# Variance plus epsilon moved from GpSimd to VectorE, with new priorities for the stages of a four-layer kernel

## The chip, the cores and the metric

The kernel runs on one core of one Trainium2 chip. The metric is device time in microseconds (us) for the whole program. The engines are named as the profile names them: PE (TensorE, matrix products), DVE (VectorE), ACT (ScalarE), POOL (GpSimd) and SP (SyncE, which here only issues DMA transfers). PEld is PE's loading of weights, which runs beside its matmuls. Each engine works through its own list of instructions in order. An instruction may wait for counters (semaphores) that other instructions raise.

## The reference

The input x has 2048 rows of 576 numbers. Four layers follow each other, attention and feed-forward twice, with the same weights both times:

```python
x = x + _A_ref(_layernorm(x), A_wqkv, A_wo)
x = x + _B_ref(_layernorm(x), B_w1, B_b1, B_w2, B_b2)
x = x + _A_ref(_layernorm(x), A_wqkv, A_wo)
x = x + _B_ref(_layernorm(x), B_w1, B_b1, B_w2, B_b2)
```

`_layernorm` is `(x - m) / sqrt(v + 1e-5)`. `_A_ref` is attention with 32 heads of 18 numbers, in which a row sees itself and the 255 rows before it, followed by the projection `wo`. `_B_ref` normalises once more, multiplies by `w1` (576 to 4608), adds `b1`, applies gelu, multiplies by `w2` (4608 to 576) and adds `b2`.

## The kernel before

**Tiles and chunks.** A tile is 128 rows. A chunk is four tiles, so each pair of an attention and a feed-forward layer has four chunks, and the program has eight, k = 0 to 7. Chunks 0 to 3 belong to the first pair, 4 to 7 to the second.

**What is done for a chunk, by stage.** A stage has a name that ends in the number of its chunk:

- `ln k`: normalises the rows for attention. DVE makes statistics (L592) and joins them to mean and variance (L594). The function `ln_rstd` then makes 1/sqrt(v + eps) in two steps: variance plus epsilon into `vtmp` (L603), and that to the power -0.5 into `rstd` (L605). DVE scales the rows (L615), and an SP transpose brings them into `xnTa` (L635).
- `q k.i`: for tile i, the products q, k and v. Each is two sets of five matmuls (L671) into two banks of PSUM; DVE copies a bank out (L710 for q and k, L697 for v), and an SP transpose brings q and k into place (L729).
- `ea k`, `eb k`: attention of the head groups 0 to 3 and 4 to 7. A group has three units. In a unit PE makes scores (L757), ACT applies exp (L766), POOL masks (L787), and PE multiplies by v (L804). At the end of a group DVE divides (L814, L819). In chunk 0 the units are smaller, since there are no rows before it.
- `t k`: the tail. An SP transpose brings the result into `attT` (L848), PE multiplies by `wo` (L671 again, a helper's line), DVE adds to `x_res` (L838), and both normalisations that follow are done in one, by the same L592 to L615, with L620 for the last 64 columns and a transpose into `xnTm` (L635).
- `ga k`, `gb k`: first and second half of the product with `w1` (L881 for the last 64 rows, L893 for the rest) and gelu on ACT (L896).
- `ma k`, `mb k`: first and second half of the product with `w2` (L922), added to `x_res` by DVE (L838), or in the last layer into the output (L841).
- Names with a `+` are the loads of `w1`, `w2` and `x_res` that belong to a stage (L536).

**What sets the order.** Nothing is emitted at once. `add` records a task with its engine, what it reads and writes, a cost, a latency and a priority. Then `Plan.schedule` places all tasks in a modelled time: of the tasks that could start first, the one with the lowest priority number goes first. It also gives each task its bank of PSUM, and before 140 us of modelled time it puts warm-up matmuls (stage without a name, function `keep_warm`) into gaps of PE. The order found so is the list that each engine works through. The dictionary `PL.nudge` adds a number to the priority of all tasks of a stage; a stage that is not in it gets nothing added:

```python
stage = self.stage + ("+" if dma in ("w1", "w2", "xr") else "")
prio += self.nudge.get(stage, 0.0)
```

So a changed entry, or a changed engine, cost or latency of any task, can move instructions everywhere in the program, on all engines and in the queues of SP and POOL.

`ln_rstd` is called with one tile (the start and the tails, 36 times) or with four (`ln`, 7 times), 43 times in all.

Of the kernel before, what the change touches and what calls it, by code (L numbers as in the profile page):

```python
# [8 lines left out]
ALU = mybir.AluOpType  # L9
# [31 lines left out]
class Sched:  # L41
# [23 lines left out]
    def add(self, eng, fn, reads=(), writes=(), dma=None, ring=4):  # L65
        waits = {}

        def want(ev):
            c, v, _e = ev
            if waits.get(c, 0) < v:  # L70
                waits[c] = v

        for r in reads:
            lw = self.last_write.get(r)
            if lw is not None and not (eng == "pe" and lw[2] == "pe"):
                want(lw)
        for w in writes:
            for rd in self.readers.get(w, ()):
                if rd[2] != eng or rd[3]:
                    want(rd[:3])  # L80
            lw = self.last_write.get(w)
            if lw is not None and not (eng == "pe" and lw[2] == "pe"):
                want(lw)
        if dma is None:
            assert eng != "sp"
            c = self.cnt[eng]
            amount = 1
        else:
            rg = self.ring(eng, dma, ring)
            c = rg.sems[rg.i % rg.k]  # L90
            rg.i += 1
            amount = 16
            if c.val > 0:
                want((c, c.val, None))
        wl = []
        wd = self.waited[eng]
        for cc, v in waits.items():
            if wd.get(cc, 0) >= v:
                continue
            wd[cc] = v  # L100
            wl.append((cc, v))
        c.val += amount
        own = None if dma is not None else eng
        ev = (c, c.val, own)
        self.steps[eng].append(Step(eng, fn, wl, c, amount))
        for w in writes:
            self.last_write[w] = ev
            self.readers[w] = []
        for r in reads:
            self.readers.setdefault(r, []).append((c, c.val, own, dma is not None))  # L110
        return ev
# [297 lines left out]
def build_kernel(nc, A_x, A_wqkv, A_wo, B_x, B_w1, B_b1, B_w2, B_b2, out):  # L409
# [32 lines left out]
    PL = Plan(S, 7)  # L442
    add = PL.add


    PL.nudge = {"b": 1.83, "ea0": -1.98, "ld0+": 40.46, "eb0": 2.23, "q1.0": -6.02, "q1.1": 1.09, "t0": 6.35, "ga0": -26.49, "q2.0": 12.46,
                "q2.2": 12.06, "q2.3": 21.72, "t1": -35.56, "ea2": -3.78, "ga1": -4.7, "ma1": 15.69, "ma1+": -9.39, "q3.2": -1.65, "q3.3": -7.2,
                "eb3": 1.74, "ma2": 3.52, "q4.0": 39.31, "q4.2": 6.69, "q4.3": -1.19, "t3": 50.91, "mb2": 75.66, "mb2+": -12.34, "eb4": 2.23,
                "ma3": 19.38, "q5.3": 4.22, "t4": -3.2, "ln6": 1.17, "ga4": 2.93, "ma4": 3.37, "q6.0": 2.8, "q6.1": 2.68, "q6.3": 11.39, "t5": 14.34,
                "gb4": 5.24, "ln7": 19.99, "ea6": 18.52, "mb4": 22.88, "ma5": 16.32, "q7.0": 16.24, "q7.1": 29.31, "q7.2": 33.42, "q7.3": 24.98,  # L450
                "t6": 73.06, "gb5": 28.24, "mb5": 74.41, "ga6": -3.51, "eb7": -2.5, "t7": -1.07}

    def sb(name, shape, dtype):
        return nc.alloc_sbuf_tensor(name, shape, dtype)
# [21 lines left out]
    vtmp = sb("vtmp", [P, NT], FP32)  # L476
# [91 lines left out]
    for i in range(NQN):  # L568
        add("pool", lambda e, i=i: e.memset(qn[:, i, :].rearrange("p (h e) -> p h e", e=32)[:, :, DH:32], 0.0),
            writes=[f"qn{i}h{h}" for h in range(2)], cost=0.5, prio=-9)  # L570
# [26 lines left out]
    def ln_rstd(ts, fused, prio):  # L597
        t0, n = ts[0], len(ts)
        var = mv_all[:, t0:t0 + n, 1]
        mvs = [f"mv{t}" for t in ts]  # L600
        rds = [f"rstd{t}" for t in ts]
        sc, bi = (1.0 + EPS, EPS * EPS) if fused else (1.0, EPS)
        add("pool", lambda e: e.tensor_scalar(vtmp[:, t0:t0 + n], var, sc, bi, op0=ALU.mult, op1=ALU.add),  # L603
            reads=mvs, writes=[f"vt{t}" for t in ts], cost=0.2, lat=0.09, prio=prio)
        add("pool", lambda e: e.tensor_tensor(rstd[:, t0:t0 + n], vtmp[:, t0:t0 + n], nhalf[:, 0:n], ALU.pow),  # L605
            reads=[f"vt{t}" for t in ts] + ["nhalf"], writes=rds, cost=0.4 + 0.155 * n, lat=0.08, prio=prio)

# [236 lines left out]
    def tail(k, prio):  # L844
        l, t0, nt = CH[k]
        rd = [f"aq{g}" for g in range(G)]
        for i in range(nt):
            add("sp", lambda e, i=i: e.dma_start_transpose(attT[:, :, i * 128:(i + 1) * 128], attq[:, i, :]),  # L848
                reads=rd + ["aqd"], writes=[f"aT{i}"], dma="t", ring=8, cost=1.3, lat=0.6, move=0.72, desc=640, prio=prio - 0.1)
        for i in range(nt):  # L850
            t = t0 + i
            bs = two_out(lambda c, i=i: attT[:, c, i * 128:(i + 1) * 128], lambda c, s: wo_sb[:, c, s:s + HB],
                         [f"aT{i}", "woA", "woB", "woC"], prio)
            for o in range(2):
                resid(t, o, bs[o], prio)
            ln_stats(t, prio)
            ln_rstd([t], True, prio)
            ln_norm_T(t, i, xnTm[:, k % 2], f"xm{k % 2}_", prio, dup=True)
# [82 lines left out]
    def ln1(k, prio):  # L941
        l, t0, nt = CH[k]
        ts = list(range(t0, t0 + nt))
        ln_rstd(ts, False, prio)
        for i, t in enumerate(ts):
            ln_norm_T(t, i, xnTa, "xa", prio)
# [5 lines left out]
    for i in range(n0):  # L952
        ln_rstd([i], False, -20)
        ln_norm_T(i, i, xnTa, "xa", -6, x_in, [f"xin{i}"], pe=True)
    add("pool", lambda e: e.memset(vA[:, :, :, DH:VW], 1.0), writes=[f"v{s}h{h}" for s in range(VS) for h in range(2)], cost=0.7, reads=["rstd3"], prio=-5)
    xin_load(4, 4, ["xa3"], -6)
    for i in range(n0):
# [4 lines left out]
        cost=0.5, prio=-1)  # L962
    dma("sp", b2bc[:, :], bass.AP(tensor=B_b2.tensor, offset=B_b2.offset, ap=[[0, P], [1, D]]), reads=["k3"], writes=["b2"], cls="b", ring=2,
        cost=0.5, prio=-1)
    add("pe", lambda e: e.transpose(bank(bb).bitcast(BF16)[:, 0:NF], b1in[:, :], ident[0:NF, 0:NF]), reads=["b1i", "ident"], writes=[bb],
        cost=0.1, lat=0.22, prio=5, alloc=[bb])
# [24 lines left out]
    for k in range(NK + 1):  # L991
        b = 4 * k
# [64 lines left out]
def bass_interleave_layers__sliding_block__mixer_channel_mlp__prompt_kernel(  # L1057
    nc,
    A_x,
    A_wqkv,  # L1060
    A_wo,
    B_x,
    B_w1,
    B_b1,
    B_w2,
    B_b2,
    out,
):
    build_kernel(nc, A_x, A_wqkv, A_wo, B_x, B_w1, B_b1, B_w2, B_b2, out)
# [28 lines left out]
```

The softmax here doesn't subtract the row's maximum and nothing guards it: scores larger than these inputs give would overflow.

## Time and profile before

| | us |
|---|---|
| median of 4 runs | 927.55 (926.53 to 928.12) |
| the profiled execution | 929.88 |
| its span, first to last instruction | 927.8 |
| PE busy | 899.6 (97%) |
| ACT busy | 598.7 (65%) |
| POOL busy | 366.8 (40%) |
| DVE busy | 317.2 (34%) |
| L603 on POOL, 36 of one tile | 209 ns each |
| L605 on POOL, 36 of one tile, 7 of four | 587 and 1022 ns each |
| mean granted clock of PE | 0.998 |

The profile is one execution. A row of a group of instructions gives line, engine, operation, what is written and read, and the count; then busy time and mean duration of one in ns; then how long the engine stood idle just before, and what ended that. A row of the timeline gives start and duration, the same names, and in brackets how long the engine had stood idle and which instruction or transfer ended the wait. Rows of equal instructions that follow each other are merged. A stretch of matmuls counts as busy even where each is short, so the waits say more than the busy share.

### The profile page before, as it was taken

The numbers are of one execution on the slowest core, as the hardware profiler recorded it, in microseconds if no ns is written. First come the engines' busy times: TensorE is split into PE (matmuls) and PEld (weight loads), VectorE is DVE, ScalarE is ACT, GpSimd is POOL, SyncE is SP. The second block draws the span as 40 slices with busy tenths as digits, with TensorE's granted clock in tenths as the row PEclk, the third lists the DMA queues.
The fourth block names the chain that finished last, engine by engine and source line by source line (L and its number), as shares of the span: only waits on it lengthen the run. The fifth ranks groups of instructions, "written<-read, shape, count | busy, mean of one in ns | idle before, by whom it ended". The sixth has DMA issues, their size and how long they took to land. (4 is left out here: it accounts for less than half of the span.)

```text
span 927.8 us, 22424 instructions
## 1 busy us (share of the span) xinstructions
PE 899.6 (97%) x9374; PEld 566.4 (61%) x9411; DVE 317.2 (34%) x797; ACT 598.7 (65%) x721; POOL 366.8 (40%) x505
## 2 busy tenths in 40 slices
PE   8989899999999999999999999999999999999998
PEld 6556465575756757577564756656576564657556
DVE  5647211841334403176020723145123420241001
ACT  4877687677836777662777667656685777852541
POOL 3766444562613626061351644315443363610100
PEclk9999999999999999999999999999999999999999
DMA  8798839934196332852739451683619626184430
GB/s 195 122 213 136 190 113 201 223 118 132 35 208 166 117 115 95 189 104 48 226 42 273 73 170 61 168 196 60 202 41 209 156 56 216 31 211 147 155 115 26
DMA packets 204596, 128.85 MB, mean 139 GB/s; under 512 B 128848, under 2 KB 202448, under 8 KB 204496
## 3 DMA queue, kind: packets, MB, share of 16 engines
q1 hardware_dynamic: 199952, 120.06, 52.4%
q0 software_dynamic: 2112, 4.72, 2.1%
q10 hardware_dynamic: 2432, 2.65, 0.9%
q8 instruction: 74, 1.21, 0.6%
q14 instruction: 26, 0.21, 0.1%
HBM read 91.87 MB, written 2.36 MB: 102 GB/s over the span
## 5 line engine op out<-in xcount | busy, mean ns | idle before, releaser
L766 ACT ACTIVATE pT<-ps 128x1024 bf16<-128x1024 f32 (+2 forms) x384 | 348.8, 970 | 123.7 <-PE ps L757 122.6
L787 POOL TENSOR_SCALAR_AFFINE_SELECT pT<-pT 128x512 bf16<-128x512 bf16 (+1 forms) x368 | 282.0, 790 | 269.4 <-ACT pT L766 260.5
L922 PE MATMUL ps<-w_sb,hT 128*128 128x288 bf16 x2304 | 313.5, 286 | 1.5 <-DVE x_res L838 1.5
L896 ACT ACTIVATE hT<-ps,b1col 128x512 bf16<-128x512 f32 x288 | 198.0, 687 | 174.6 <-PE ps L893 173.0
L893 PE MATMUL ps<-xnTm,w_sb 128*128 128x512 bf16 x1115 | 255.0, 379 | 3.0 <-issue 1.7
L922 PEld LDWEIGHTS ps<-w_sb,hT 128*128 128x128 bf16 x2304 | 211.9, 97 | 71.3 <-issue 16.7
L893 PEld LDWEIGHTS ps<-xnTm,w_sb 128*128 128x128 bf16 x1152 | 108.8, 98 | 138.0 <-issue 17.4
L838 DVE TENSOR_TENSOR x_res<-ps,x_res 128x288 f32<-128x288 f32 x160 | 71.3, 450 | 235.3 <-PE ps L922 213.3
L671 PE MATMUL ps<-wqkv,xnTa 128*128 128x288 bf16 x960 | 135.9, 288 | 5.9 <-DVE qn L710 2.5
L671 PEld LDWEIGHTS ps<-wqkv,xnTa 128*128 128x128 bf16 x960 | 87.2, 98 | 39.8 <-DVE qn L710 7.6
L804 PEld LDWEIGHTS ps<-vA,pT 128*128 128x128 bf16 x2880 | 94.1, 96 | 25.7 <-POOL pT L787 12.2
L804 PE MATMUL ps<-vA,pT 128*128 128x20 bf16 x2880 | 100.0, 171 | 4.1 <-POOL pT L787 3.5
L710 DVE CAST qn<-ps 128x288 bf16<-128x288 f32 x120 | 54.2, 454 | 117.4 <-PE ps L671 116.9
L904 POOL TENSOR_TENSOR x_res<-x_res,b2bc 128x576 f32<-128x576 f32 x32 | 40.9, 1277 | 115.5 <-ACT hT L896 115.4
L757 PE MATMUL ps<-qT,kT 32*128 32x384 bf16 (+2 forms) x1216 | 64.2, 277 | 3.9 <-ACT pT L766 2.7
L814 DVE RECIPROCAL rinv<-ps 128x16 f32<-128x16 f32 x64 | 16.2, 253 | 129.1 <-PE ps L804 128.9
L603 POOL TENSOR_SCALAR vtmp<-mv_all 128x1 f32<-128x1 f32 (+1 forms) x43 | 8.9, 206 | 109.4 <-DVE mv_all L594 107.9
L592 DVE BATCH_NORM_STATS2 st_all<-x_res 128x6 f32<-128x288 f32 x104 | 44.8, 448 | 11.6 <-DMA x_res<-in_A_x_dram 10.1
L671 PE MATMUL ps<-wo_sb,attT 128*128 128x288 bf16 x320 | 45.0, 286 | 1.7 <-DMA attT<-attq 0.9
L881 PE MATMUL ps<-xnTm,w_sb 64*128 64x512 bf16 x288 | 39.5, 377 | 2.4 <-DMA xnTm<-xn 1.4
L615 DVE TENSOR_SCALAR xn<-x_res,mv_all,rstd 128x576 bf16<-128x576 f32 x52 | 36.6, 705 | 13.8 <-DMA xnTm<-xn 8.0
L757 PEld LDWEIGHTS ps<-qT,kT 32*128 32x128 bf16 x1216 | 19.5, 92 | 34.5 <-issue 18.6
(43 smaller groups left out, 284.7 us busy)
## 6 DMA issues: line engine op xcount, KB each, us to landing
w_sb<-in_B_w_dram SPq DMA_DIRECT2D x48, 864.0 KB, 6.2
w_sb<-in_B_w_dram SPq DMA_DIRECT2D x48, 768.0 KB, 4.8
w_sb<-in_B_w_dram SPq DMA_DIRECT2D x96, 48.0 KB, 4.6
x_res<-in_A_x_dram POOLq DMA_DIRECT2D x4, 1152.0 KB, 7.3
out_dram<-xn SPq DMA_DIRECT2D x16, 144.0 KB, 1.8
wqkv<-in_A_wqkv_dram ACTq DMA_DIRECT2D x3, 576.0 KB, 7.5
hT<-in_A_x_dram SPq DMA_DIRECT2D x2, 576.0 KB, 5.4
wo_sb<-in_A_wo_dram ACTq DMA_DIRECT2D x1, 576.0 KB, 6.6
```

The costliest lines, as they stand in the source:

```text
L592: add("dve", lambda e, i=i, s=s: e.bn_stats(st_all[:, t, i, :], s[:, t, i * HB:(i + 1) * HB]), reads=res, writes=[f"st{t}_{i}"], cost=0.37 ...
L671: ins = e.matmul(bank(bs[o])[:, 0:HB], lhs(c), rhs(c, o * HB), start=(c == 0), stop=(c == KD - 1))
L710: add("dve", lambda e, b=bs[o], dst=dst: e.tensor_copy(dst, bank(b)[:, 0:HB].rearrange("p (h d) -> p h d", d=DH)), reads=[bs[o]], writes=[ ...
L757: ins = e.matmul(two(bs[j // 2])[:, j % 2, col:col + nq * 128], k_of(T0 + so)[0][32 * j:32 * j + 32, g, :], qs[32 * j:32 * j + 32, g, qo * ...
L766: add("act", lambda e, h2=h2: e.activation(pT[:, sl, 2 * h2:2 * h2 + 2, lo:hi], two(bs[h2])[:, :, lo:hi], ACT.Exp, scale=SCALE), reads=[bs ...
L787: add("pool", lambda e, ap=ap, pat=pat, sgn=sgn, kind=kind: e.affine_select(ap, ap, pattern=pat, compare_op=(ALU.is_ge if kind == "d" else ...
L804: ins = e.matmul(bank(B_O)[:, o:o + VW], pT[:, sl, j, col + qi * 128:col + (qi + 1) * 128], vA[:, (T0 + so) % VS, 4 * g + j, :], start=(fi ...
L838: add("dve", lambda e: e.tensor_tensor(x_res[:, t, sl], bank(b)[:, 0:HB], x_res[:, t, sl], ALU.add), reads=[b], writes=[f"x{t}h{hh}"], cos ...
L893: ins = e.matmul(bank(bk)[:, 0:n], w1_sb[:, sl, col:col + 128], xnTm[:, k % 2, c, 0:n], start=False, stop=(c == 3))
L896: add("act", lambda e, ff=ff, fl=fl, bk=bk: e.activation(hT[:, fl, 0:n], bank(bk)[:, 0:n], ACT.Gelu_apprx_tanh, bias=b1col[:, ff:ff + 1]), ...
L904: add("pool", lambda e, t=t: e.tensor_tensor(x_res[:, t, :], x_res[:, t, :], b2bc[:, :], ALU.add), reads=["b2", f"h{fl}"], writes=X(t), co ...
L922: ins = e.matmul(bank(b)[:, 0:HB], hT[:, fl, i * 128:(i + 1) * 128], w2_sb[:, fl, hh * HB:(hh + 1) * HB], start=(fl == 0), stop=(fl == NFH ...
```

## The change

`ln_rstd` computes variance plus epsilon on DVE instead of POOL, with a modelled cost of 0.1 instead of 0.2 and a latency of 0.14 instead of 0.09. POOL keeps the power. And `PL.nudge` has other entries: 43 instead of 55.

```diff
-    PL.nudge = {"b": 1.83, "ea0": -1.98, "ld0+": 40.46, "eb0": 2.23, "q1.0": -6.02, "q1.1": 1.09, "t0": 6.35, "ga0": -26.49, "q2.0": 12.46,
...
-                "t6": 73.06, "gb5": 28.24, "mb5": 74.41, "ga6": -3.51, "eb7": -2.5, "t7": -1.07}
+    PL.nudge = {"b": 2.99, "ea0": 3.17, "q1.0": 4.26, "q1.1": 4.31, "q1.2": 4.01, "q1.3": 3.37, "ga0": -2.67, "q2.0": 14.64, "q2.1": 2.99,
...
+                "eb6": 0.91, "ma5": 10.07, "q7.1": -1.18, "q7.3": 7.71, "ea7": -15.2, "ga6": -19.72, "eb7": -2.14}
```

```diff
         sc, bi = (1.0 + EPS, EPS * EPS) if fused else (1.0, EPS)
-        add("pool", lambda e: e.tensor_scalar(vtmp[:, t0:t0 + n], var, sc, bi, op0=ALU.mult, op1=ALU.add),
-            reads=mvs, writes=[f"vt{t}" for t in ts], cost=0.2, lat=0.09, prio=prio)
+        add("dve", lambda e: e.tensor_scalar(vtmp[:, t0:t0 + n], var, sc, bi, op0=ALU.mult, op1=ALU.add),
+            reads=mvs, writes=[f"vt{t}" for t in ts], cost=0.1, lat=0.14, prio=prio)
         add("pool", lambda e: e.tensor_tensor(rstd[:, t0:t0 + n], vtmp[:, t0:t0 + n], nhalf[:, 0:n], ALU.pow),
             reads=[f"vt{t}" for t in ts] + ["nhalf"], writes=rds, cost=0.4 + 0.155 * n, lat=0.08, prio=prio)
```

The list of each engine changes in many places, up to a point near the end: the last 190 steps of PE are the same in both.

## The prediction

> **What bounds the kernel now.** I read the page first, then who PE waits for, then PE's timeline, and last PE against the other engines in chosen windows. The page says that PE is the bound:
>
> ```profile
> span 927.8 us, 22424 instructions
> PE 899.6 (97%) x9374; PEld 566.4 (61%) x9411; DVE 317.2 (34%) x797; ACT 598.7 (65%) x721; POOL 366.8 (40%) x505
> ```
>
> 927.8 less 899.6 leaves 28 us. The change adds and removes no matmul of the computation, so an order can win only from these 28 us, and lose by making more of them. Who PE waits for, longest in total first:
>
> ```profile
> PE ps L757 <- ACT pT L766: 4.1, 12, 1.1
> PE ps L804 <- POOL pT L787: 3.5, 8, 1.1
> PE ps L671 <- DVE qn L710: 2.8, 4, 1.2
> PE ps L671 <- DMA xnTa<-xn: 2.4, 1, 2.4
> ...
> PE ps L922 <- DVE x_res L838: 1.5, 5, 0.6
> PE ps L881 <- DMA xnTm<-xn: 1.4, 1, 1.4
> ...
> PE ps L671 <- DMA attT<-attq: 0.9, 1, 0.9
> ...
> PE ps L757 <- DVE mv_all L594: 0.8, 1, 0.8
> ```
>
> Columns: total, times, longest. They are small and many; none is a wait for rstd. Where they lie is seen in PE's timeline:
>
> ```profile
> 40.67 0.34 PE L757 MATMUL ps<-qT,kT 32*128 32x384 bf16 x4
> ...
> 45.08 0.34 PE L757 MATMUL ps<-qT,kT 32*128 32x384 bf16 x4
> ...
> 48.58 0.79 PE L671 MATMUL ps<-wqkv,xnTa 128*128 128x288 bf16 x5 [2.42 <-DMA xnTa<-xn]
> ...
> 53.45 0.34 PE L757 MATMUL ps<-qT,kT 32*128 32x384 bf16 x4 [0.16 <-ACT pT L766]
> ...
> 101.90 0.82 PE L881 MATMUL ps<-xnTm,w_sb 64*128 64x512 bf16 x6 [1.44 <-DMA xnTm<-xn]
> ```
>
> The windows show the same start with the granted clock (columns after the stretch: its length, then busy time of PE, PEld, DVE, ACT, POOL, then clock, DMA share, GB/s):
>
> ```profile
> 30.00:33.60 3.60, 2.65 (x56) 1.82 (x54) 3.15 (x11) 2.61 (x4) 1.28 (x3) 1.00 0.82 129
> 33.60:37.00 3.40, 3.29 (x28) 1.72 (x25) 1.97 (x8) 3.02 (x5) 2.64 (x5) 0.51 0.49 81
> 46.00:48.60 2.60, 0.18 (x3) 0.02 (x2) 0.46 (x1) 0.98 (x2) 2.11 (x4) 1.00 1.33 380
> ```
>
> In one stretch of 3.4 us the clock was 0.51: 3.29 us of PE work there would have taken half, so 1.6 us were lost. It follows a stretch in which PE had mostly short matmuls (36 of the 56 are L804, of 20 columns).
>
> **The moved operation.** Its chain, once, at the start:
>
> ```profile
> 4.44 0.21 DVE L594 BATCH_NORM_AGGREGATE mv_all<-st_all 128x2 f32<-128x12 f32 x1
> 4.73 0.19 POOL L603 TENSOR_SCALAR vtmp<-mv_all 128x1 f32<-128x1 f32 x1 [0.43 <-DVE mv_all L594]
> 5.01 0.56 POOL L605 TENSOR_TENSOR rstd<-vtmp,nhalf 128x1 f32<-128x1 f32 x1
> ```
>
> From the end of the aggregate (4.65) to the start of the power (5.01) 0.36 us pass. After, VectorE follows itself, which took 0.04 us between statistics and aggregate; then come its operation and a hop of 0.08 to GpSimd (4.65 to 4.73). VectorE's operation on 128x1 is not in the trace. Nearest rows:
>
> ```profile
> L603 POOL TENSOR_SCALAR vtmp<-mv_all 128x1 f32<-128x1 f32 x36 | 7.5, 209 | 90.2 <-DVE mv_all L594 89.0
> L594 DVE BATCH_NORM_AGGREGATE mv_all<-st_all 128x2 f32<-128x12 f32 x64 | 12.8, 200 | 0.7
> ```
>
> Below, VectorE's memset of 165 ns; above, its reciprocal of 253 ns. I take 0.20, the nearest in size: 0.04 + 0.20 + 0.08 = 0.32 instead of 0.36, so 0.04 us less per chain (0.075 less to 0.01 more). If all 43 chains lay on PE's path, that would be 1.7 us; no PE wait ends at rstd, so I count nothing: each chain is covered by fill matmuls, or ends in a late transpose priced below. GpSimd gets 8.9 us free of 367, and waits for ACT in long stretches anyway (L787: 260.5 us). Its power still stands in line behind masks, so in chains of four tiles (masks to 23.84 us, then L603 at 23.92) only the 0.28 us of L603 and its hop go. VectorE gets 43 x 0.20 = 8.6 us on top of 317: its 34% become 35%. What is queued behind the new instruction on VectorE are the evictions of PSUM banks. PE waited for VectorE some 12 times in about 440 evictions, so 43 x 12/440 x 0.2 = 0.2 us; with the gain on a few chains, this part is 0 (-1.7 to +1).
> [...]
>
> **The new order.** I counted PE's list in both programs. The work prices: five L671 matmuls 0.61 us (x30 from 14.05 to 17.78), six L922 0.74, four L893 0.86, scores of a unit 0.24 to 0.34, its L804 0.19 to 0.39, 0.09 for changing away from scores. By them the two lists weigh the same to half a us. Warm-up matmuls are 46 in both. SP issues the same 152 transposes (1.2 us each in its timeline) and 215 copies in another order; no PE wait ends at a weight load, and I price that at nothing: the least cover is 6.6 us of PE work between the release of a w2 slice and its first use (7.0 before), against 4.8 us to landing on the page; late, it would cost what lies above 6.6. The last 190 PE steps (from 784 us on) are the same. So the sum is one of waits.
>
> *Up to the first feed-forward block (101.9 us).*
> Goes: the 2.42 at 48.58 (from the last read of its tile of xnTa to the first use there were 3 units and 3 sets of L671, 3.85 us; now 24.8). The 1.44 at 101.90 (8.7 us of work after the last L671 of the tail; now 15.2): -3.86.
> Comes: the transpose for tile 2 of chunk 2 has 2.88 us of work to hide in (2 units, 2 sets). Before, 4.54 us were enough with no wait, and 3.85 were 2.42 short, so it needs at most 4.5 or as much as 6.3: 0 to 3.4 us. The first attT of the tail is in the same place with 4.1 us; it needed 4.18 + 0.89 = 5.07 in chunk 2, and its wait lies in the same time. PE is held up by ACT there too, so I take 1.5.
> Comes: attention of chunk 0 is thinner. Sets of L671 among the scores of head groups 1 to 7 were 3, 3, 3, 5, 5, 3, 4; now 1, 2, 3, 4, 3, 3, 3. PE work per group falls from 3.9 to 5.1 us to 2.5, 3.2, 4.3, 4.4, 4.2, 3.8, 3.8. The quickest group took 4.41 us (40.67 to 45.08, with 4.0 of work), so exp and masks allow about 4.4. After lacks 1.9 + 1.2 + 0.1 + 0 + 0.2 + 0.6 + 0.6 = 4.6, before 1.3. The first group of chunk 1 falls to 4.7, where the quickest full-size group took 6.18: +1.2. Net +4.5. Were the floor that of the groups of 5.8 us, it would be some 6 more; nothing less, since 4.41 is the best seen.
> Goes with it: 0.80 and 0.37 in chunk 0, now inside that floor, and half of the 0.31, 0.31, 1.15, 1.13 in chunk 1, which has 30 sets instead of 29 there: -2.6.
> Clock: group 1, with one set, is thinner than the stretch that brought 0.51; I take one such stretch again: 0 (-1.6 to +3.2).
> Sum -0.5.
> [...] Here the longest wait before the fall was 0.80, and the 2.42 us were followed by 1.00. [...]
>
> *From there to 784 us.*
> Goes, each where the list has changed: 0.89 (attT, 261.8), 0.99 (638.1), 0.59 (178.5), 0.37 (402.1), 0.51, 0.33, 0.30 (masks): -3.98.
> Comes: tile 1 of chunk 5 now has 2.93 us between the last read of xnTa and first use: 4.54 - 2.93 = 1.6 (0 to 3.4). The first tile of chunk 4 has 12.40 us from its last residual; 13.21 were 0.99 short in chunk 7, 12.42 were enough in chunk 5: 0.9 (0 to 1.8). Banks that come back late: +0.3. Mask waits fall where units meet little fill, and the list has as many such places: +1.1. Sum -0.1.
>
> Together -0.6. The profiled execution took 929.88 us (927.8 and 2.1 around), 2.3 above the median of 927.55; the difference is put on the median: **926.9**.
>
> **Rivals.** (a) *Slower: the clock falls more often.* Groups 1 and 2 of chunk 0 (about 30 to 40 us) and 6 to 8 (about 55 to 70) are thin in the new list. Every half-clock stretch with PE at the bound costs 1.6. Three more give 926.9 + 4.8 = 931.7; two more decide it (930.1). For: the one fall came after thin work. Against: ACT has PE waiting there anyway, and similar waits at 46 and 90 us cost no clock. (b) *Faster: the thin groups cost nothing*, because the start was late by chains, not by ACT: the -3.9 stay, +4.5 shrinks to 1: 923.4. Against: groups 3 and 6 stood at 4.4 and 4.7 with less PE work. (c) *The operation is no faster on VectorE*: 0.01 more per chain, nothing to see; the order alone decides, so this is inside all cases.
>
> **How the numbers follow.** Even exchange (924 to 930) 0.42; (a), 930 to 936, 0.33; (b), 919 to 924, 0.25. About 0.2%, 1.9 us, can be told from no change here: faster is below 925.7, slower above 929.4. Faster: 0.25 and 0.10 of the first; slower: 0.33 and 0.08; the rest 0.24. The range takes most of both sides, 920 to 935.
>
> **What would show it.** No PE wait at the second chunk's first L671, none of 1.4 at the first L881; waits of 1 to 2 at q2.2 (about 75 us) and at tile 1 of chunk 5 (about 450 us); L766 as the releaser of PE in 30 to 40 and 55 to 70 us; L603 on VectorE at about 0.2 us. Wrong if the first L881 starts far from 98 us, if the clock row has two or more stretches of 0.5, or if weight loads on SP's queue are waited for.

## The result and the profile after

| | before | after |
|---|---|---|
| median, us | 927.02 (46 runs, 924.53 to 929.98) | 930.93 (28 runs, 926.74 to 934.99) |
| after / before | | 1.0038 [1.0029, 1.0046] |
| profiled execution, its span, us | 929.88, 927.8 | 931.23, 929.4 |
| mean granted clock (before: 85 executions timed beside the experiments; after: its 28) | 0.9989 | 0.9943 |

The changed kernel is slower by 0.38%, where 926.9 us and an even exchange were forecast. 930.93 lies inside the range, on the side to which 0.41 had been given. The profiled execution of before was one of its longer ones: 929.88 against a median of 927.02. Lines of the changed kernel stand one lower than before (L671 is L670, L757 L756, L766 L765, L615 L614, L603 L602).

The page of after, with the span first and then the busy times:

```profile
span 929.4 us, 22415 instructions
PE 899.6 (97%) x9373; PEld 567.5 (61%) x9411; DVE 323.2 (35%) x840; ACT 598.1 (64%) x721; POOL 355.9 (38%) x462
PEclk9899999999999999999999999999999999999999
```

PE is still the bound. VectorE has 43 instructions and 6 us more, GpSimd 43 and 11 us less. The clock row has an 8 in the second slice, 23 to 46 us. The operation itself, in the groups of after (busy time, mean of one in ns):

```profile
L602 DVE TENSOR_SCALAR vtmp<-mv_all 128x1 f32<-128x1 f32 x36 | 5.2, 143 | 0.5
L602 DVE TENSOR_SCALAR vtmp<-mv_all 128x4 f32<-128x4 f32 x7 | 2.3, 328 | 0.2
```

It takes 143 ns where 200 were priced. Who PE waits for in after (total, times, longest):

```profile
PE ps L756 <- ACT pT L765: 4.9, 16, 0.6
PE ps L670 <- DVE qn L709: 4.4, 7, 2.3
...
PE ps L670 <- DMA attT<-attq: 1.8, 3, 1.3
PE ps L803 <- POOL pT L786: 1.6, 4, 0.7
PE ps L803 <- DVE attq L818: 1.5, 2, 1.2
...
PE ps L670 <- DMA xnTa<-xn: 1.1, 2, 0.8
```

The 2.4 for `xnTa` and the 1.4 for `xnTm` are gone, as forecast, and so is most of the wait for masks. Waits for exp rose from 4.1 to 4.9. One row was not forecast: PE waits for VectorE's copies of `qn`, once for 2.3 us. PE's timeline of after places the waits:

```profile
39.06 0.34 PE L756 MATMUL ps<-qT,kT 32*128 32x384 bf16 x4 [0.28 <-ACT pT L765]
41.68 0.99 PE L670 MATMUL ps<-wqkv,xnTa 128*128 128x288 bf16 x5 [2.28 <-DVE qn L709]
...
79.50 2.01 PE L670 MATMUL ps<-wo_sb,attT 128*128 128x288 bf16 x15 [1.33 <-DMA attT<-attq]
...
99.48 0.82 PE L880 MATMUL ps<-xnTm,w_sb 64*128 64x512 bf16 x6
...
458.12 3.83 PE L670 MATMUL ps<-wqkv,xnTa 128*128 128x288 bf16 x30 [0.76 <-DMA xnTa<-xn]
```

What VectorE does while PE stands still, from its timeline in after:

```profile
37.02 0.69 DVE L614 TENSOR_SCALAR xn<-hT,mv_all,rstd 128x576 bf16<-128x576 bf16 x1
37.63 0.44 DVE L818 TENSOR_TENSOR attq<-ps,rinv 128x288 bf16<-128x288 f32 x1
38.00 3.26 DVE L614 TENSOR_SCALAR xn<-hT,mv_all,rstd 128x576 bf16<-128x576 bf16 x3
41.18 0.44 DVE L709 CAST qn<-ps 128x288 bf16<-128x288 f32 x1
```

And GpSimd's in the same stretch:

```profile
38.39 0.97 POOL L535 DMA_DIRECT2D x_res<-in_A_x_dram  x1 [0.84 <-PE ps L756]
39.38 3.54 POOL L786 TENSOR_SCALAR_AFFINE_SELECT pT<-pT 128x1024 bf16<-128x1024 bf16 x5
```

Of the three scalings merged in the row at 38.00, the first two took 414 and 417 ns. The third started at 38.67, inside GpSimd's issue of the first `x_res` load, and took 2581 ns. The copy of a `qn` bank stood behind it on VectorE, and PE waited for that bank. In before the load stood at 42.21, behind the last scaling (41.02 to 41.76), and none of the four there took over 0.84 us.

The windows of after, cut at the half-clock stretches (columns as before):

```profile
30.00:35.30 5.30, 3.17 (x47) 1.78 (x44) 4.65 (x17) 5.30 (x8) 3.50 (x5) 1.00 0.74 101
35.30:38.70 3.40, 3.40 (x55) 1.96 (x52) 2.31 (x7) 2.20 (x4) 2.51 (x4) 0.50 0.42 82
38.70:42.10 3.40, 0.84 (x11) 0.45 (x9) 2.92 (x3) 2.26 (x4) 3.38 (x5) 1.00 0.70 171
42.10:45.50 3.40, 3.40 (x43) 2.27 (x42) 1.08 (x3) 0.96 (x2) 0.83 (x2) 0.50 1.03 253
```

Two stretches of 3.4 us at half clock where before had one: the first behind the thin head groups (PE busy 3.17 of 5.30 us), the second behind the stalled VectorE (0.84 of 3.40). A half-clock stretch of 3.4 us lowers the mean clock of a whole execution by 3.4 x 0.5 / 928 = 0.0018. So by the mean clocks an average execution of before has 0.0011 / 0.0018 = 0.6 such stretches, and one of after 3.2.

### The profile page after: what moved, and what is told of

Its sections match the earlier page's. It is cut to its first block, busy times and chain, and to the rows that moved or that the text cites. A ratio compares the mean times of both kernels' runs of the same rounds, so it can differ in the third digit from the quotient of the medians.

```text
span 929.4 us, 22415 instructions
## 1 busy us (share of the span) xinstructions
PE 899.6 (97%) x9373; PEld 567.5 (61%) x9411; DVE 323.2 (35%) x840; ACT 598.1 (64%) x721; POOL 355.9 (38%) x462
## 4 chain that ended last, share of the span: by engine, by line
PE 82%; DMA 6%; DVE 4%; issue 3%; ACT 2%; POOL 2%; SPq 0%; POOLq 0%; DVEq 0%
PE ps L921 26%; PE ps L892 26%; PE ps L670 14%; PE ps L803 7%; PE ps L756 5%; PE ps L880 4%; ACT pT L765 2%; DMA xnTm<-xn 2%; DMA attT<-attq 1%; POOL pT L786 1%; DMA xnTa<-xn 1%; DMA hT<-in_A_x_dram 1%; DVE st_all L591 1%; DVE xn L614 1%; DVE x_res L837 1%
## 5 line engine op out<-in xcount | busy, mean ns | idle before, releaser
L765 ACT ACTIVATE pT<-ps 128x1024 bf16<-128x1024 f32 (+2 forms) x384 | 348.5, 970 | 134.7 <-PE ps L756 133.4
L670 PE MATMUL ps<-wqkv,xnTa 128*128 128x288 bf16 x960 | 136.7, 288 | 6.8 <-DVE qn L709 4.4
L670 PEld LDWEIGHTS ps<-wqkv,xnTa 128*128 128x128 bf16 x960 | 87.2, 98 | 40.7 <-DVE qn L709 8.3
L709 DVE CAST qn<-ps 128x288 bf16<-128x288 f32 x120 | 54.0, 454 | 102.4 <-PE ps L670 100.1
L604 POOL TENSOR_TENSOR rstd<-vtmp,nhalf 128x1 f32<-128x1 f32 (+1 forms) x43 | 27.6, 642 | 130.9 <-DVE vtmp L602 130.6
L756 PE MATMUL ps<-qT,kT 32*128 32x384 bf16 (+2 forms) x1216 | 64.6, 278 | 5.5 <-ACT pT L765 4.0
L670 PE MATMUL ps<-wo_sb,attT 128*128 128x288 bf16 x320 | 45.6, 286 | 1.8 <-DMA attT<-attq 1.8
L696 DVE CAST vA<-ps 128x288 bf16<-128x288 f32 x64 | 28.9, 455 | 39.1 <-PE ps L670 38.8
L756 PEld LDWEIGHTS ps<-qT,kT 32*128 32x128 bf16 x1216 | 19.4, 92 | 36.0 <-issue 19.2
L880 PE MATMUL ps<-xnTm,w_sb 64*128 64x512 bf16 x288 | 39.5, 377 | 1.8 <-ACT pT L765 0.4
```

The source lines that it names most:

```text
L670: ins = e.matmul(bank(bs[o])[:, 0:HB], lhs(c), rhs(c, o * HB), start=(c == 0), stop=(c == KD - 1))
L709: add("dve", lambda e, b=bs[o], dst=dst: e.tensor_copy(dst, bank(b)[:, 0:HB].rearrange("p (h d) -> p h d", d=DH)), reads=[bs[o]], writes=[ ...
L756: ins = e.matmul(two(bs[j // 2])[:, j % 2, col:col + nq * 128], k_of(T0 + so)[0][32 * j:32 * j + 32, g, :], qs[32 * j:32 * j + 32, g, qo * ...
L765: add("act", lambda e, h2=h2: e.activation(pT[:, sl, 2 * h2:2 * h2 + 2, lo:hi], two(bs[h2])[:, :, lo:hi], ACT.Exp, scale=SCALE), reads=[bs ...
L880: ins = e.matmul(bank(bk)[:, 0:n], w1_sb[64 * b:64 * b + 64, sl, col:col + 128], xnTm[64 * b:64 * b + 64, k % 2, 4, 0:n], start=True, stop ...
```

## The experiments

The theories on record are T1: the loss is made in the start, by VectorE's evictions that come late and by the falling clock; T2: it is spread over the new order behind 102 us; T3: the operation itself costs it. In the experiments' kernels, line numbers are a few higher or lower than in the kernel that they were made from; the rows name what is written, so that L614 is known by `xn<-hT` and L709 by `qn<-ps`. Each ratio is to the kernel before, timed in the same round: 33 executions beside experiments 1, 2, 3 and 5 (median 927.32 us), 35 beside 4 and 6 to 8 (927.32), 17 beside 9 to 11 (926.39).

**1. The new order, the operation on GpSimd.** A slot in the task names another engine at emission, so that the lists stay those of after.

```diff
-                self.S.add(t.eng, t.fn, ...
+                self.S.add(t.emit or t.eng, t.fn, ...
-        add("dve", lambda e: e.tensor_scalar(vtmp...
+        moved = add("dve", lambda e: e.tensor_scalar(vtmp...
+        moved.emit = "pool"
```

> The new lists unchanged, but variance plus epsilon goes back to GpSimd at the place it has in the new order. Theory 1 (the loss is made in the start of the new order, by a late DVE and a falling clock): no change against the new kernel, 930 to 931.5, ratio to before 1.003 to 1.005. Theory 2 (the loss is spread over the order behind 102 us): the same. Theory 3 (the operation itself costs, queued in front of evictions on VectorE): 927 to 928, ratio 1.000 to 1.001.

Measured: 929.53 us (12 runs), ratio 1.0017 [1.0003, 1.0032], mean clock 0.9942. The new order is slower without the moved operation too. The collision is there again: three scalings in 4.42 us from 37.99 (the third 3742 ns), and the clock was at 0.50 from 36.1 to 46.3. The time lies between what T3 (927 to 928) and T1 (930 to 931.5) expected. T3 doesn't explain this run; 0.2% of the 0.38% is left unaccounted for, with intervals that overlap.

**2. The first load of `x_res` later.** In after, only the load is moved, six GpSimd steps down its list (the expectation says five), to 46.94.

```diff
+        at = next(i for i, x in enumerate(order) if x[1].eng == "pool" and x[1].dma)
+        x = order.pop(at)
+        later = [i for i, y in enumerate(order) if i >= at and y[1].eng == "pool"]
+        order.insert(later[5] + 1, x)
```

> The new kernel with one step moved: GpSimd issues the first load of x_res behind five more masks, so it no longer lies beside the scaling of chunk 2's rows (L614), one of which took 2.58 us beside it instead of 0.41. Theory 1: that L614 takes 0.4 to 0.8 us, the wait of 2.28 us of PE at 41.7 us goes, and with it one stretch at half clock: 927 to 928.5, ratio 1.000 to 1.002. Theory 2: 930 to 931, and the profile shows the start shorter but the rest longer by its old 2 us. If the long L614 came from the masks and not from the load, it stays long.

Measured: 928.09 us (12 runs), ratio 1.0006 [0.9989, 1.0024], mean clock 0.9963. The three scalings, in VectorE's timeline of this kernel:

```profile
38.79 1.10 DVE L618 TENSOR_SCALAR xn<-hT,mv_all,rstd 128x576 bf16<-128x576 bf16 x3
```

1.10 us instead of 3.26, and PE's longest wait for `qn` falls from 2.3 to 0.7. Moving one transfer gives back 2.8 of the 3.9 us. The mean clock rises by 0.0020, one half-clock stretch on average, but is not that of before.

**3. The same load earlier in the kernel before.** In its list the load goes three masks up, from 42.21 to 38.08, right behind the output of the second head group.

```diff
+        at = next(i for i, x in enumerate(order) if x[1].eng == "pool" and x[1].dma)
+        x = order.pop(at)
+        order.insert(next(i for i, y in enumerate(order) if "aq1" in y[1].writes) + 1, x)
```

> The kernel before with one step moved: GpSimd issues the first load of x_res three masks earlier, beside the scaling of chunk 2's rows (L615). Theory 1: one L615 takes 2 to 2.6 us instead of 0.4 to 0.8, VectorE's evictions behind it are late, and PE waits 1 to 2.3 us more near 41 us, perhaps with one more stretch at half clock: 928 to 931, ratio 1.001 to 1.004. Theory 2 (such a collision has no weight): 926.5 to 927.5, ratio 0.9995 to 1.0005.

Measured: 928.99 us (12 runs), ratio 1.0015 [1.0000, 1.0031], mean clock 0.9977. VectorE's timeline of this kernel:

```profile
37.69 0.41 DVE L618 TENSOR_SCALAR xn<-hT,mv_all,rstd 128x576 bf16<-128x576 bf16 x1
38.02 0.44 DVE L700 CAST vA<-ps 128x288 bf16<-128x288 f32 x1
38.39 3.20 DVE L618 TENSOR_SCALAR xn<-hT,mv_all,rstd 128x576 bf16<-128x576 bf16 x2
```

The first of the two scalings at 38.39 starts inside the load (38.08 to 39.04) and takes 2542 ns. So the collision can be made in the old order too. Its cost there, 1.4 us by the ratio, has an interval that begins at 0, and it shows in the clock: none of the 12 executions was at a mean clock of 1.0 (before: 16 of 33), while at 0.998 its median is 928.99 and that of before 929.29. The copy from PSUM at 38.02 ran into the load at its usual 0.44.

**4. What holds the scaling.** In after, the load goes two masks up, to 36.24, and loses its wait for the second head group, so that it lies beside the first scaling.

```diff
+        x = order.pop(at)
+        x[1].reads = ()
+        order.insert([i for i, y in enumerate(order) if i < at and y[1].eng == "pool"][-2], x)
```

> The change, with GpSimd's first load of x_res two masks earlier, right behind the power (and without its wait for the second head group), so at about 36.4 us: it now lies beside the first L614 scaling operation, not the third. Tells what holds the scaling. If a scaling that starts inside the load is held until GpSimd pauses: the first scaling (start about 37.0) takes 1.4 to 1.8 us, until the two masks behind the load are done at about 38.5, and the third takes 0.42; the evictions behind lose 1 us, time 928 to 930. If the load alone holds it: 0.6 to 0.8 us, and time 927.5 to 928.5. If it is the masks beside the third scaling, and not the load: the third is still near 2.5 us, and time 930 to 931.

Measured: 928.98 us (12 runs), ratio 1.0020 [1.0003, 1.0036], mean clock 0.9947. VectorE's timeline of this kernel:

```profile
36.33 0.99 DVE L618 TENSOR_SCALAR xn<-hT,mv_all,rstd 128x576 bf16<-128x576 bf16 x1
37.24 0.44 DVE L822 TENSOR_TENSOR attq<-ps,rinv 128x288 bf16<-128x288 f32 x1
37.60 2.82 DVE L618 TENSOR_SCALAR xn<-hT,mv_all,rstd 128x576 bf16<-128x576 bf16 x3
```

And GpSimd's:

```profile
36.24 0.97 POOL L539 DMA_DIRECT2D x_res<-in_A_x_dram  x1
37.23 4.96 POOL L790 TENSOR_SCALAR_AFFINE_SELECT pT<-pT 128x512 bf16<-128x512 bf16 x7
```

None of the three expectations fits alone. The first scaling ended 0.10 us after the load did (986 ns): the load alone holds it. Of the three behind, which ran beside masks without a gap, one took 1783 ns and one 731: masks alone hold it as well, the longer one past a change from mask to mask. All the scalings of `hT` rows (bf16) of over 0.9 us in the traces ended 0.08 to 0.23 us behind the start of a GpSimd instruction. So it looks as if such a scaling gets through where GpSimd changes from one instruction to the next, and it can miss that place: not at all here (986 ns), once (1783), twice (2581 and experiment 3's 2542), four times in experiment 1 (3742). In after it ended at 41.26, 0.23 us behind the start of a mask that took 715 ns where its like take 625 to 642. This is a reading of the times that no run tests; the scalings of `x_res` rows (f32, 576 columns) of over 0.9 us, 19 in before and after, ended later behind such a start, 15 of them by 0.35 to 0.36 us and the others by 0.95 to 1.41. The part of the load in after is twofold: it holds the scaling, and it pushes the masks behind it into one unbroken row of five.

What waits here is VectorE, for GpSimd, and one wait can last over several GpSimd instructions (2581 and 3742 ns). The first scaling did not stand still to the end of the load: it would then have ended its own 0.34 us or more behind it, and it ended 0.10 behind (986 ns). Why VectorE waits, no run here shows.

**5. More PE work in the thin part, on the path.** In after, six sets of the second chunk's first tile are computed twice (their result is the same, since the second pass starts the bank anew).

```diff
+        reps = 2 if PL.stage in ("q1.0",) else 1
-                for c in range(KD):
+                for c in list(range(KD)) * reps:
```

> The new kernel, with each of the six sets of five L670 matmuls of stages q1.0 done twice (the second overwrites the first with the same values), so that PE streams more in the thin groups of chunk 0; 3.7 us more PE work. Theory 1 with the clock as its cause: at most one stretch of half clock in the profile, and 927.5 to 930 in spite of the added work, ratio 1.000 to 1.003. If the clock is not the cause, the added work lies partly on the path: 931 to 934, ratio 1.004 to 1.008, with the same number of stretches.

Measured: 933.14 us (10 runs), ratio 1.0053 [1.0035, 1.0070], mean clock 0.9968. The clock rose from 0.9943, as theory T1 has it, but the added 3.7 us of work and a longer collision (a scaling of 3748 ns) cost more. By the letter of the expectation it is the other case: 931 to 934 us, with two half-clock stretches in the profile, as in after; only the mean over the executions speaks for T1. So the next run puts the work where PE waits.

**6. Filler where PE waits, load out of the way.** On top of experiment 2: behind each product of chunk 0's head groups 1 to 4 that isn't its group's last, four matmuls of zeros go to unused columns of the same bank.

```diff
+            for r in range(4 if k == 0 and g < 4 and not last else 0):
+                ins = e.matmul(bank(B_O)[:, 320:512], warm[:, 0:128], warm[:, 0:192], start=False, ...
```

> after_load_later, with matmuls of zeros on 192 unused columns of the attention's bank behind the first products of head groups 1 to 4 of chunk 0 (four behind each one that isn't a group's last): they lie where TensorE waits for the exponentials, 0.32 us each four, some 2.5 us in all between 28 and 47 us. If the thin stretch makes the clock fall: fewer half-clock stretches, mean granted clock 0.998 or above (after_load_later 0.9963), time 926 to 927.5, ratio 0.9985 to 1.0000. If the clock falls whatever TensorE streams there: clock as before, 0.994 to 0.997, and time 928 to 930.5, the filler being paid in part.

Measured: 927.95 us (12 runs), ratio 1.0006 [0.9992, 1.0020]. The mean clock was 1.0 in 11 of 12 executions, 0.9998 over all. The windows of experiment 2's kernel:

```profile
32.00:36.00 4.00, 1.99 (x25) 1.12 (x26) 3.66 (x15) 3.74 (x6) 3.29 (x6) 0.76 0.66 71
36.00:40.00 4.00, 3.92 (x56) 2.25 (x54) 2.46 (x8) 2.31 (x3) 2.25 (x4) 0.50 0.36 70
40.00:44.00 4.00, 3.80 (x45) 2.34 (x46) 0.71 (x2) 2.26 (x5) 3.25 (x5) 0.50 0.34 66
```

And with the filler:

```profile
32.00:36.00 4.00, 2.88 (x49) 2.02 (x50) 3.74 (x14) 3.37 (x6) 3.29 (x5) 1.00 0.28 51
36.00:40.00 4.00, 2.92 (x48) 1.54 (x46) 3.11 (x8) 3.37 (x5) 2.95 (x5) 1.00 0.34 66
40.00:44.00 4.00, 3.36 (x57) 2.48 (x58) 1.75 (x5) 2.35 (x4) 2.22 (x4) 1.00 0.35 68
```

With 0.9 us more of PE work in the 4 us of 32 to 36, the clock stayed. None of experiment 2's 12 executions was at 1.0. So in this order the thin stretch is what lets it fall: that part of T1 is shown. The time, 927.95, lies between the two ranges; it did not follow, and the next run shows why.

**7. The same filler in the kernel before.** The edit is that of experiment 6.

> The kernel before with the same filler. If the thin stretch makes the clock fall: nearly all executions at a mean clock of 1.0 (before: half of them), time lower by 0.5 to 1 us less what of the filler lies on the path, ratio 0.9985 to 1.0005. If not: the same mix of clocks, and ratio 1.0005 to 1.0025.

Measured: 930.05 us (12 runs), ratio 1.0029 [1.0013, 1.0045], mean clock 0.9990, with 1.0 in 6 of 12 executions (before: 50 of 85). The expectation from the thin stretch, nearly all at 1.0, failed here. At equal clock the filler costs 928.89 - 926.29 = 2.6 us (medians of the executions at 1.0): all of its 2.5 us lies on the path. It did not help before's clock: in its profile the half-clock stretch no longer stands at 33.66 but at 49.15, behind the wait for `xnTa` (1.9 us here), which the filler does not fill. By that price the order of experiment 2 at full clock would take some 927.93 - 2.6 = 925.3 us; its own median is 928.09. So its clock costs it about 2.8 us (an estimate from these two runs). Its own executions point to the same: 926.75 us at a mean clock of 0.998 (six) and 929.60 at 0.994 (four) lie on a line that reaches 925.3 at 1.0.

**8. and 9. The operation alone.** The kernel before with its own lists, and only the operation emitted on VectorE.

```diff
+        moved = add("pool", lambda e: e.tensor_scalar(vtmp...
+        moved.emit = "dve"
```

> The kernel before with its own order on every engine; only the variance operation goes from GpSimd to VectorE. Theory T3 (the operation itself costs the time): most of the 3.5 us of the change show here, 929 to 930.5 us, ratio 1.002 to 1.004. Theory T1 (the loss is made in the start, by the order that the new priorities give it): nothing to see, ratio 0.999 to 1.001, the operation about 0.15 us on VectorE, no wait of TensorE for the eviction near 41 us, and no fall of the clock beyond the kernel before's.

Measured: 925.00 us (12 runs), ratio 0.9977 [0.9959, 0.9995]. No theory had a gain, so it was run again:

> before_dve_op once more, since it came out 2.3 us below the kernel before, which no theory had, with an interval that ends near 1. If the operation by itself gains (its price off the power's chain, 4 to 8 tiles' normalisation earlier, the 2.4 us wait for the second chunk's transposes gone): ratio 0.9965 to 0.9990 again, and two thirds or more of the executions at a clock of 1.0. If that was the luck of one set of executions: ratio 0.9990 to 1.0005.

Measured: 925.07 us (12 runs), ratio 0.9982 [0.9964, 1.0000]; 17 of the 24 executions at a clock of 1.0. This version has the lowest median of all, though the second interval touches 1. At a mean clock of 1.0 the medians are 924.65 us here and 926.29 before, 1.6 apart. T3 falls: by itself the operation gains about 2 us on an order that was not made for it. Two rows from PE's timeline of experiment 8. The second set of five in the first row is the one that waited 2.42 us at 48.58 in before:

```profile
43.93 1.40 PE L673 MATMUL ps<-wqkv,xnTa 128*128 128x288 bf16 x10
...
98.51 0.82 PE L883 MATMUL ps<-xnTm,w_sb 64*128 64x512 bf16 x6 [1.03 <-DMA xnTm<-xn]
```

PE no longer waits for a transfer into `xnTa`: neither profile of this kernel has such a wait, where before had one of 2.42 and experiment 7, on the same order, one of 1.9. But experiment 3, on the same order and with the operation on GpSimd, has none either. What differs is how long the transpose took from issue to landing, first before (issued at 41.81), then experiment 8 (at 40.29):

```profile
xnTa<-xn SPq DMA_TRANSPOSE x1, 6.7
xnTa<-xn SPq DMA_TRANSPOSE x1, 2.6
```

In before its last packets moved among those of the first `x_res` load (44.11 to 48.19); in experiment 8 all had started by 42.40, and the load's first came at 42.53. Whether the operation decides this or chance is not settled. PE reaches the first feed-forward block at 98.51 instead of 101.90; up to 1.7 of these 3.4 us are the half-clock stretch that before's profiled execution had and this one lacks. From there to the end it takes another 1.5 us less. One part of that is seen in every profile of the old order: between 635 and 639 us PE waits once for 0.82 to 0.99 us, behind VectorE, with the operation on GpSimd (before, 3 and 7), and in the same matmuls at most 0.24 us with it on VectorE (8 and 9).

**10. New priorities for the start, old ones behind**, operation on VectorE, everything planned anew.

> The change's operation on VectorE, with the new priorities for the steps up to the third tile set of chunk 2 and the old ones behind: TensorE's first 236 steps are the changed kernel's, so its collision of load and scaling and its thin groups are in it. T1 (the start makes the loss): 929 to 931.5 us, ratio 1.002 to 1.0045, mean clock 0.993 to 0.996, a scaling of 2.5 us or more near 39 us. T2 (the order behind makes it): 925 to 927 us, ratio 0.998 to 1.000.

Measured: 940.32 us (6 runs), ratio 1.0138 [1.0108, 1.0168], mean clock 0.9933. Both theories missed. The expected collision did not come about: VectorE's three scalings ran before the load could hold them.

```profile
37.28 1.09 DVE L610 TENSOR_SCALAR xn<-hT,mv_all,rstd 128x576 bf16<-128x576 bf16 x3
```

The load was issued at 37.67 and took 1.02 us. The third scaling started 0.28 us into it and was not held (0.42 us); in after and in experiment 1 it started 0.28 us into the load and was held, in experiment 3 even at 0.32. So the moment of the start doesn't tell which of the two goes first; what does is open. PE reached the first feed-forward block at 96.28, the earliest of all runs, with the same thin groups. What was lost came behind: waits of the first w1 matmuls for exp add up to 4.9 us, the longest 2.3. Old priorities on a plan that has changed are worth little, so this run does not separate T1 from T2. It does say that the thin groups alone are not dear in a profile with one half-clock stretch in the start, and that the collision doesn't come every time.

**11. All old priorities, operation on VectorE, planned anew.** The diff is the change without its new `PL.nudge`.

> The operation on VectorE in the planner's list too, with the old priorities: the change without its new priorities. The planner then reorders the start by itself; GpSimd's first load of x_res comes right behind the second head group's output, with the four scalings behind it in VectorE's order, so the collision is expected here as well. If the collision is what decides: one scaling of 1.5 to 3.7 us near 38 to 41 us, time 928 to 931, ratio 1.001 to 1.004. If the new priorities are what costs, whatever collides: 925 to 927, ratio 0.998 to 1.000.

Measured: 972.31 us (6 runs), ratio 1.0483 [1.0452, 1.0514], mean clock 0.9785. The collision is there: four scalings in 4.39 us.

```profile
40.18 4.39 DVE L610 TENSOR_SCALAR xn<-hT,mv_all,rstd 128x576 bf16<-128x576 bf16 x4
```

But it is a small part of 46 us. Most is a plan that no longer fits, with waits for exp of 12.0 and 11.2 us in two groups (4.1 for the first in before) and a window like this:

```profile
560.00:584.00 24.00, 15.41 (x269) 7.91 (x269) 3.15 (x10) 20.66 (x23) 16.89 (x23) 0.58 0.01 2
```

So the same operation, with the same old priorities, gives 925 us where only the engine is exchanged, and 972 where the planner sees it. New priorities were needed once the task was changed for the planner; they won back 41 of 46 us, and not the rest.

**Start or rest.** The first w1 product divides PE's list. Ahead of it the new list has four sets of L671 less (20 matmuls, 2.4 us) and one unit of L804 more with its change away from the scores (0.5 us by the prediction's prices), so 2.0 us of work have gone behind it. For the new list, these 2.0 us are added to the first column and taken from the second, so that the rows can be compared:

| profiled execution | first w1 product starts, us | from there to the end, us | half-clock stretches of 3.4 us |
|---|---|---|---|
| before | 101.9 | 825.9 | 1 |
| load earlier in before (3) | 101.2 | 826.5 | 1 |
| operation alone (8) | 98.5 | 824.4 | 0 |
| operation alone, again (9) | 98.5 | 824.6 | 0 |
| after | 101.5 | 827.9 | 2 |
| new order, operation on GpSimd (1) | 103.5 | 825.5 | 3 |
| load later (2) | 102.2 | 824.9 | 3 |
| load early (4) | 101.3 | 825.8 | 2 |

Against the operation alone, the new order loses 2.8 to 5.0 us in the start. Behind it, its four executions lose 0.4 to 3.4 us, 1.5 on average. So most of the loss is made in the start, as T1 has it; T2 has a part, which these few executions don't size.

**What the 3.9 us are made of**, from medians: the operation alone -2.0 (925.0 against 927.0); the collision +2.8 (930.9 against 928.1, of which one half-clock stretch is a part); what is left, 928.1 - 925.0 = 3.1, is mostly the clock that falls in the thin groups (about 2.8 by experiment 7, less 0.4 that the operation alone loses by its own clock: 925.07 against 924.65 at full clock). Some 0.7 us stays with the rest of the order; which waits make it was not settled.

## Why the prediction was wrong, point by point

- **The clock, "I take one such stretch again: 0".** This is the term that failed first. It was sized from one execution of before, which had one stretch, and what was wrong is the number of such stretches: 50 of 85 executions of before had none, and after has three on average. Relative to the medians the term should have been about (3.2 - 0.6) x 1.1 = 2.9 us, not 0 (1.1 us a stretch: over after's 28 executions the time rises by 0.59 us for 0.001 of clock). Its own upper bound was 3.2, and rival (a), with "three more", gave 931.7. So half-clock stretches behind thin work were rival (a)'s mechanism, and its chance was set too low; one of them came behind the collision, which no rival had.
- **The collision was not priced at all.** SP's transposes were counted past each other, but a moved load on GpSimd's queue was not: from 42.21 to 38.39, with four scalings of VectorE moved forward against it. It brought the 2.28 us wait at 41.68, and the clock was at 0.50 from 42.10 to 45.50. So the term was left at nothing, and in experiment 2, moving the load alone gave back 2.8 us. The two terms overlap by the one half-clock stretch that goes with the collision, some 1.1 us.
- **The thin groups, +4.5.** Too dear by what is seen: PE's waits for exp between 24 and 75 us rose from 1.0 to 2.6 us, and experiment 10 reached the first feed-forward block at 96.28 with the same groups. The floor itself was there: from the end of one group to the end of the next, the last three of chunk 0 took 4.69 us each in after, with ACT busy 4.4 to 4.6 of them, where 4.41 was taken. Why the sum of the lacks came out too high was not worked out. Rival (b) was nearer in this step; that the same thinness pays through the clock was the other half.
- **The start's sum of -0.5** came out by luck. In the profiles the first L880 came 2.4 us earlier (99.48 against 101.90), with 2.0 us less PE work ahead of it, so -0.4. But that holds one more half-clock stretch (1.7 us) and the 2.28 us wait, neither in the sum; they made up for what was too dear. "The two lists weigh the same" held for the whole, not for its halves. Behind the start the forecast was -0.1; this execution took 2.0 us more than before's, three others on the new order 0.1 to 1.0 less.
- **The moved operation, 0.** It measured 143 ns instead of 200, and alone it gave about -2 us, just outside the stated -1.7 to +1. "No PE wait ends at rstd" was true and misled: with the operation moved, and nothing else, a wait of 0.8 to 1.0 us near 638 us went, though the profile of before puts it down to VectorE's copy of `qn`. Why it went, and what makes the rest of the gain was not settled. The 0.20 was too dear for the 128x1 form alone; the 128x4 form took 328 ns on average in after (169 to 611) and 104 to 170 in experiments 8 and 9.
- **Right:** the waits of 2.42 and 1.44 went; `attT` waits 1.33 us at 79.50 (1.5 were taken for this wait and one that may coincide with it); tile 1 of chunk 5 waits 0.76 (1.6 taken). The wait named as possible for tile 2 of chunk 2, near 75 us, did not come. A weight load was waited for once, by 0.4.
- **The base.** The 2.3 us by which the profiled execution lay above the median were put on the median unexplained. By the clocks they are mostly its half-clock stretch: executions of before at 0.998 have a median of 929.34, those at 1.0 one of 926.29. To keep that stretch in the sum as "0" and start from the median of 927.55 left it out of the forecast.
- **The windows ahead of the clock's falls.** In after the clock fell at 35.3 behind a window in which PE was busy 3.17 of 5.30 us and waited for 0.57 at most at a time, and at 42.1 behind one with PE busy 0.84 of 3.40, with the wait of 2.28. With 0.9 us more work in 4 it did not fall (2.88 us against 1.99, experiments 6 and 2). So a window that was only thinly filled was enough here, without a long wait, as it had been in before at 33.66; each stretch at half clock lasted 3.4 us.

## What to carry to other kernels

A moved instruction must be looked at against every engine that it could share something with, and a DMA issued by GpSimd is an instruction of GpSimd: here a load issued 4 us earlier held an SBUF-to-SBUF operation of VectorE (2581 ns where its like took 414 and 417), the PSUM copies behind it and PE (2.28 us), and a stretch of 3.4 us at half clock followed. Read the clock of many executions before taking one profile as the base, since executions of before with about one half-clock stretch and with none lay 3.0 us apart, beside an effect of 3.9. And measure the edit on an unchanged order (only the engine exchanged when the list is emitted) apart from its new plan: here the edit gained 0.2%, and the plan that came with it lost 0.6%.

## What the runs showed of the hardware that was not expected

- A scaling of 128x576 bf16 from SBUF to SBUF on VectorE took 341 to 423 ns beside an idle GpSimd (experiment 2), up to 837 beside a mask in before and up to 1783 beside masks without a gap, and 2542 to 3748 where it was held by GpSimd's issue of a DMA with masks right behind. Copies out of PSUM kept their 443 ns beside the same load (experiments 3 and 10).
- PE's clock fell to half with PE busy 1.99 of 4 us (experiment 2) and stayed at full with 2.88 of 4 (experiment 6), but busy time alone does not decide it. In before, PE was busy for longer in the first of these two stretches, and only this one was followed by half clock:

```profile
30.25:33.66 3.41, 2.46 (x55) 1.68 (x54) 3.21 (x11) 2.42 (x4) 1.23 (x2) 1.00 0.88 138
98.51:101.92 3.41, 1.97 (x21) 1.37 (x19) 1.37 (x3) 3.18 (x4) 2.92 (x4) 1.00 1.24 137
```

  They differ in what PE worked on. The first has 36 matmuls of L804 (20 columns, 1.13 us) and 12 of scores (L757, on 32 of the 128 rows, 0.68 us) beside 7 of L671 (288 columns, 0.94 us); in the second, 15 of L671 make 1.95 of the 1.97 us. Whether that decides it was not tested.
- One program, executed again and again, had half-clock stretches in some executions and none in others: medians of before were 926.29 us at a mean clock of 1.0 and 929.34 at 0.998. That is 3.0 us for a stretch that, at half clock for 3.4 us, costs 1.7 by itself (an estimate); what the other 1.3 us are stays open, since no profile of before at full clock was at hand.
